# A soft mixture of experts that combines from the dispatch's own exponentials, strip by strip

## The chip, the cores and the metric

The kernel runs on one core of one Trainium2 chip. The metric is the device time of one launch in microseconds (us), as a median over several runs; lower is better. The engines that matter here are TensorE (PE in the profile, its weight loads PEld), VectorE (DVE), ScalarE (ACT), GpSimd (POOL) and the sync engine's queue (SP), which issues nearly all DMA transfers.

## The reference

Attention with a window of 96 keys, 8 global keys and a linear distance bias, for 4 batches, 8 heads, 768 positions and head width 64, makes `x` of 3072 tokens by 512. The second half is a soft mixture of experts with 8 experts of 4 slots each:

```python
logits = x @ phi                              # [3072, 32]
d = np.exp(logits - logits.max(0, keepdims=True))
d /= d.sum(0, keepdims=True) + 1e-09          # dispatch: per slot, over tokens
slot_input = d.T @ x                          # [32, 512]
for e in range(E):
    h = np.maximum(slot_input[e] @ w1[e], 0.0)
    slot_out[e] = h @ w2[e]                   # [32, 512] in all
c = np.exp(logits - logits.max(1, keepdims=True))
c /= c.sum(1, keepdims=True) + 1e-09          # combine: per token, over slots
return c @ slot_out                           # [3072, 512]
```

Both softmaxes are taken over the same logits, once along each axis.

## The kernel before

**Order.** Everything is issued from one flat program. The attention phase is the list `ORDER` (L56), a hand-written order of small steps that are looked up by name and called one after the other (L845); each engine takes its instructions in that order. Behind it `last_dispatch` (L763), the expert layers and the combine follow in plain program order. Weights stream in through SP (`load_w`, L397) into 2,048-column places, as soon as what lay there is used up.

**Attention.** Sixteen units (batch, pair of heads) pass through scores, bias, exponential, a split into two fp16 parts, values and division. `tr` (L624) transposes the output, and `logits` (L647) multiplies it by `phi`.

**Strips.** The logits of one batch stand on the 128 partitions as four strips of 32 slots: strip `s` holds tokens `240 s` to `240 s + 239`, so `lsb` is 128 by 240 (the last strip has 48 tokens). Each batch ends with `strip_max`, `strip_exp` and `strip_sum` (L688 to L708): a running maximum per partition, `ex = exp(lsb - max)` with its sum, and the rescaling of earlier sums. `by_token` (L716) transposes both `ex` and the raw logits `lsb` into tokens by slots, 120 tokens at a time; `by_token_copy` moves the first for the dispatch, and `lnat_copy` (L729) keeps the second in `lnat` (120 by 32 groups by 32 slots) for the combine. `dispatch` (L740) accumulates `d.T @ x` per strip in `sacc`.

**Last dispatch.** For the last batch the same steps run without cover. The strips' maxima are brought together per slot (`m4`, `ft`), `zn` holds the factors that fold the four strips and normalise, and two groups of matmuls (L814) give the slots' inputs, which `put_slots` (L104) places in `sl`. Small filler matmuls (`warm`, L773) stand between.

**Experts.** `hidden` (L110) runs twice, for experts 0 to 3 and 4 to 7, four experts side by side in 32-column groups; VectorE and ACT meanwhile run `softmax` (L154) over `lnat` and `split` (L166), which lays each weight out twice, as an F32R part and its remainder. `hidden_t` (L126) transposes the hidden rows, `weights_by_slot` (L175) transposes the split weights into `ct` (128 by 3072), and `check_inputs` (L860) works out whether the fast path's assumptions on the inputs hold. `project` (L141) multiplies by `w2`, for the two halves of 256 output columns one after the other, each over experts 0 to 3 and 4 to 7. Its result has 4 experts in 32-row groups, and each slot's row stands several times; `slots_out` (L191) folds the sign pattern `sgn` into an F32R part and a remainder, so that one matmul with `ct` gives the full product. `set_flag` (L879) sums the checks by a matmul into a flag that a branch at the end reads (L939); if it is set, a general path recomputes everything.

**Combine.** `Moe.combine` (L197) takes 128 tokens at a time: one F32R matmul of 128 rows by 256 columns (L209), two of them to a PSUM bank, evacuated in turn by ACT (L212) and VectorE (L214), and written to HBM in pieces of 4 tiles (512 KB) from six output buffers used in rotation. PSUM tiles of this stage rotate through six banks (`LeftBanks`, L500). The end of the program is

```python
    project(0, 0)
    project(0, 1)
    slots_out(0)
    set_flag()
    project(1, 0, range(3))
    combine(0, 0, (4,) * 5)
    project(1, 0, range(3, 8))
    project(1, 1)
    slots_out(1)
    combine(0, 20, (4,))
    combine(1, 0, (4,) * 6)
```

## Time and profile before

| what | value |
|---|---|
| median of 3 runs | 214.49 us (213.32 to 215.28) |
| the profiled execution | 213.26 us |
| its span, first to last instruction | 211.5 us |
| PE busy | 182.5 us, 86% |
| DVE / ACT / POOL busy | 150.8 / 127.6 / 116.0 us |
| moved by DMA | 61.40 MB, mean 290 GB/s |
| written to HBM | 6.29 MB |

The span is shorter than the profiled execution's own time by what lies around it. Times inside the span are counted from its start. The page's strip of 40 slices gives the busy share of 5.3 us each in tenths; that of TensorE shows it busy through nearly the whole span and idle in the last two slices:

```profile
PE   8679799986999989999999998887699999998400
```

In a row of the costliest groups the order is: line, engine, operation, output and inputs by the program's names, shapes, count, then busy time and the mean time of one in ns, then the engine's idle time ahead of them and what ended it. A piece of the chain of waits is: start, length, engine, tile and line, and the number of instructions merged in it. A window's row is: its ends and length, busy time of PE, PEld, DVE, ACT and POOL with counts, the granted TensorE clock, the mean share of the DMA engines, and GB/s. A matmul in fp32 shows as two records, an F32R matmul or a transpose as one.

### The profile page before, as it was taken

Reading aid. Unit: us, or ns where it says so; the run is one execution under the profiler, and the core shown is the slowest. Engines: PE = TensorE matmul, PEld = TensorE weight load, DVE = VectorE, ACT = ScalarE, POOL = GpSimd, SP = SyncE. Lnnn points to the kernel's source line nnn. Section 1 sums busy time; section 2 is a strip of 40 time slices with the busy share of each in tenths; the row PEclk is TensorE's granted clock in tenths of the full one; section 3 lists DMA queues with packets and bytes.
Section 4 is the critical chain, followed back from the end, with each engine's and each line's share of the span. In section 5 each row is a group of like instructions: output and inputs, shape, how many; then the busy total and the mean of one; then the engine's idle time right before and its main releaser. Section 6 shows DMA issues by size and latency. Waiting matters only on the chain.

```text
span 211.5 us, 6475 instructions
## 1 busy us (share of the span) xinstructions
PE 182.5 (86%) x2649; PEld 131.8 (62%) x2649; DVE 150.8 (71%) x375; ACT 127.6 (60%) x177; POOL 116.0 (55%) x141
## 2 busy tenths in 40 slices
PE   8679799986999989999999998887699999998400
PEld 2357688765787868878788876656253366576300
DVE  4889999658889878989988999296567835153600
ACT  2429899919589768979799989642403552042400
POOL 8436989785799796998889999840000000000000
PEclk9999999998899999999999999699999999999955
DMA  4769999997998976663487678998998999459892
GB/s 115 295 193 396 397 381 380 319 343 282 336 398 314 354 291 222 240 236 118 153 276 243 223 248 248 354 373 309 369 384 275 385 397 388 163 188 315 285 337 91
DMA packets 21063, 61.40 MB, mean 290 GB/s; under 512 B 2336, under 2 KB 9376, under 8 KB 19360
## 3 DMA queue, kind: packets, MB, share of 16 engines
q1 hardware_dynamic: 20880, 60.89, 79.8%
q8 instruction: 23, 0.38, 0.7%
q14 instruction: 16, 0.13, 0.2%
q10 hardware_dynamic: 144, 0.00, 0.0%
HBM read 54.59 MB, written 6.29 MB: 288 GB/s over the span
## 4 chain that ended last, share of the span: by engine, by line
PE 49%; DMA 18%; DVE 15%; POOL 9%; issue 3%; ACT 1%; DVEq 0%; POOLq 0%; SPq 0%
DMA wa<-in_v_dram 11%; PE x L602 11%; PE sc L538 9%; PE a L149 7%; PE hp L119 7%; POOL wa L586 6%; DVE wa L527 4%; PE m L631 3%; DMA wa<-in_qk_dram 3%; DVE wa L548 3%; PE m L736 2%; DMA out_dram<-wa 2%; DMA nraw<-in_n_dram 2%; POOL wa L519 2%; PE m L661 2%
## 5 line engine op out<-in xcount | busy, mean ns | idle before, releaser
L586 POOL TENSOR_TENSOR wa<-wa 128x432 f16<-128x432 f32 x91 | 98.4, 1111 | 12.3 <-ACT wa L578 8.1
L538 PE MATMUL sc<-wa 64*128 64x216 f32 (+2 forms) x448 | 49.3, 347 | 3.6 <-DVE mx L548 2.2
L602 PE MATMUL x<-wa 128*128 128x65 f16 (+1 forms) x1248 | 45.9, 196 | 3.5 <-POOL wa L586 2.0
L602 PEld LDWEIGHTS <-wa 128*128 128x128 f16 x1248 | 41.7, 99 | 9.6 <-issue 5.2
L578 ACT CAST wa<-wa 128x1296 f16<-128x1296 f32 x31 | 39.3, 1266 | 9.1 <-PE x L602 8.2
L538 PEld LDWEIGHTS sc<-wa 64*128 64x128 f32 x448 | 37.6, 190 | 10.6 <-DVE mx L548 4.1
L568 ACT ACTIVATE wa<-wa,nb 128x1296 f32<-128x1296 f32 x32 | 43.5, 1374 | 0.5
L548 DVE CUSTOM_DVE_ANT_1 wa<-sc,wa,mx 128x864 f32<-128x864 f32 x32 | 35.6, 1114 | 3.5 <-PE sc L538 1.0
L527 DVE SCALAR_TENSOR_TENSOR wa<-wa 128x896 f16<-128x896 f32 x16 | 24.3, 1519 | 5.5 <-ACT wa L522 3.1
L548 DVE CUSTOM_DVE_ANT_1 wa<-sc,wa 128x864 f32<-128x864 f32 x16 | 16.8, 1051 | 2.6 <-POOL wa L586 1.9
L636 ACT COPY wa<-m 128x480 f32<-128x480 f32 (+1 forms) x32 | 14.3, 473 | 6.7 <-PE m L631 6.7
L212 ACT COPY wa<-cp 128x512 f32<-128x512 f32 x12 | 6.3, 596 | 17.0 <-PE cp L209 15.3
L619 DVE CUSTOM_DVE_ANT_1 xn<-x,rc 120x448 f32<-120x448 f32 x24 | 14.9, 622 | 0.7
L522 ACT ACTIVATE wa<-wa 128x896 f16<-128x896 f32 x8 | 7.6, 951 | 11.4 <-DMA wa<-in_v_dram 10.5
L631 PE MATMUL m<-ident,xn 120*128 120x120 f32 x84 | 12.9, 276 | 1.1 <-DVE xmax L619 0.5
L519 POOL TENSOR_SCALAR wa<-wa 128x896 f16<-128x896 f32 x8 | 7.5, 941 | 10.7 <-DMA wa<-in_v_dram 8.4
L631 PEld LDWEIGHTS m<-ident,xn 120*128 120x128 f32 x84 | 8.6, 140 | 3.2 <-ACT wa L636 1.5
L119 PE MATMUL hp<-wp,sl 128*32 128x512 f32 x96 | 10.5, 593 | 0.0
L661 PE MATMUL m<-wa,phis 128*32 128x240 f32 (+1 forms) x128 | 9.5, 332 | 0.2 <-ACT wa L636 0.2
L214 DVE COPY wa<-cp 128x512 f32<-128x512 f32 x12 | 7.5, 682 | 2.1 <-PE cp L209 1.2
L609 DVE TENSOR_TENSOR rsall<-x,eps 120x7 f32<-120x7 f32 x32 | 5.0, 157 | 5.3 <-PE x L602 4.9
L561 PEld LDWEIGHTS m<-mm,bsel 2*128 2x128 f32 x32 | 4.7, 182 | 5.6 <-DVE mm L558 3.1
(163 smaller groups left out, 207.8 us busy)
## 6 DMA issues: line engine op xcount, KB each, us to landing
wa<-in_qk_dram SPq DMA_DIRECT2D x15, 832.0 KB, 6.6
wp<-in_w_dram SPq DMA_DIRECT2D x12, 1024.0 KB, 7.9
wa<-in_v_dram SPq DMA_DIRECT2D x16, 448.0 KB, 3.9
out_dram<-wa SPq DMA_DIRECT2D x12, 512.0 KB, 5.6
wp<-in_w_dram SPq DMA_DIRECT2D x8, 512.0 KB, 7.3
wp<-in_w_dram SPq DMA_DIRECT2D x16, 256.0 KB, 5.7
wa<-in_w_dram SPq DMA_DIRECT2D x3, 432.0 KB, 4.9
wa<-in_w_dram SPq DMA_DIRECT2D x1, 1024.0 KB, 6.8
```

The lines of the kernel that those rows point to most:

```text
L119: nc.tensor.matmul(out=hp[n][32 * s:32 * s + 32, :], lhsT=slv(a, c, s), rhs=w1(e, c // 2)[:, (c % 2) * DF + 512 * n:(c % 2) * DF + 512 * n ...
L149: nc.tensor.matmul(out=o[32 * s:32 * s + 32, 0:w], lhsT=ht[:, c, 32 * s:32 * s + 32], rhs=w2(4 * a + s, half)[:, c0 + c * w:c0 + c * w + w ...
L527: nc.vector.scalar_tensor_tensor(out=vlo[k].rearrange(flat), in0=vraw.rearrange(flat), scalar=V_SC, in1=vhi[k].rearrange(flat)[:, :, 0:D], ...
L538: nc.tensor.matmul(out=sc[:, i, at:at + n], lhsT=r_[r, KCOL[j]:KCOL[j] + KR], rhs=r_[r, KW + KB * j:KW + KB * j + n], start=True, stop=True)
L548: nc.vector.tensor_tensor_reduce(out=tbs[u % NTB].rearrange("p (i c) -> p i c", i=2)[:, :, BW * k:BW * k + BW], in0=scs.pop((u, k))[:, :, ...
L568: nc.scalar.activation(out=head(u, i), in_=head(u, i), func=AF.Exp, bias=nbs[u], scale=T_SC)
L578: nc.scalar.copy(out=h, in_=t)
L586: (engine or nc.gpsimd).tensor_tensor(out=w, in0=t, in1=h, op=ALU.subtract)
L602: nc.tensor.matmul(out=x[:, (D + 1) * t:(D + 1) * t + d], lhsT=w[:, c:c + P], rhs=vv[:, j, i, 0:d], start=(z == 0), stop=(z == len(ops) - ...
L619: nc.vector.tensor_tensor_reduce(out=xnb[(u // 2) % 3][:, :, c:c + D], in0=out_of(u, i)[:, :, 0:D], in1=rcs.pop((u, i)).unsqueeze(2).to_br ...
L631: nc.tensor.transpose(out=m[:, at:at + KB], in_=xnb[(u // 2) % 3][:, t, P * (p % 2):P * (p % 2) + P], identity=ident[0:KB, 0:KB])
L636: nc.scalar.copy(out=xtb[u % 3][:, a:a + n], in_=ms.pop((u, k))[:, 0:n])
```

## The change

The combine no longer has weights of its own. The exponentials `ex` of every batch are kept (`exs`, one strip tile of 128 by 240 for each batch), with the running maxima in `amax`. In `last_dispatch` the maximum over all partitions is found (`gmax`, through one transposing matmul and a reduce, and spread to all partitions by another matmul), each batch's strips are scaled by `exp(amax - gmax)` in place, and eight matmuls with a 128 by 4 selector `quad` give each token's sum over the 32 slots; their reciprocals `crec` later divide the output. Softmax by token, `split`, `weights_by_slot`, `ct` and `lnat` go. `slots_out` becomes two half copies by VectorE and ACT, and a new `slots_spread` multiplies by a permutation matrix `perm` so that every row group of 32 holds the 32 slots. The combine then takes each batch's strips as they stand: seven fp32 matmuls with 32 rows, one for each group of 120 tokens, four of them in different row groups and different PSUM banks. The evacuation multiplies by the reciprocals: VectorE for strips 0 and 2, ACT for strips 1 and 3. There are eight output buffers, one for each half and batch. `check_inputs` tests the sums in place of the softmax, and moves from behind `weights_by_slot` to behind the second `slots_spread`, with `set_flag` after it.

```diff
-    lnat = keep.tile([KB, 8 * B, NS], F32, name="lnat")
+    amax = keep.tile([P, B], F32, name="amax")
+    exs = [keep.tile([P, SW], F32, name=f"ex{b}") for b in range(B)]
...
+        nc.gpsimd.memset(quad, 0.0)
+        for k in range(4):
+            nc.gpsimd.memset(quad[32 * k:32 * k + 32, k:k + 1], 1.0)
+        nc.gpsimd.tensor_copy(out=perm.rearrange("p (r s k) -> p r s k", r=4, s=4), in_=ident.rearrange("p (s r k) -> p r s k", r=4, s=4))
...
     def by_token(b):
         ms[b, "d"] = m = bank()
-        to_tokens(m, ex, 0)
-        to_tokens(m, lsb, 2 * P)
+        to_tokens(m, exs[b], 0)
...
         strip_max(last)
         strip_exp(last)
-        ml = tile()
-        to_tokens(ml, lsb, 2 * P)
+        top = amax[:, b:b + 1]
+        nc.tensor.matmul(out=mt[0:1, 0:P], lhsT=top, rhs=ident, start=True, stop=True)
         warm()
...
+        nc.vector.tensor_reduce(out=gmax, in_=mt[0:1, 0:P], axis=AX.X, op=ALU.max)
+        nc.tensor.matmul(out=mt[:, P:P + 1], lhsT=ones[0:1, :], rhs=gmax, start=True, stop=True)
         for s in range(4):
             nc.vector.tensor_reduce(out=ft[32 * s:32 * s + 32, 0:1], in_=m4, axis=AX.X, op=ALU.max)
...
         by_token_copy(last)
-        ms[b, "d"] = ml
-        lnat_copy(last)
+        nc.vector.tensor_tensor(out=fs[:, 0:B], in0=amax, in1=mt[:, P:P + 1].to_broadcast([P, B]), op=ALU.subtract)
+        nc.scalar.activation(out=fs[:, B:], in_=fs[:, 0:B], func=AF.Exp)
+        for i in range(B):
+            f = fs[:, B + i:B + i + 1]
+            if i == 1:
+                nc.gpsimd.tensor_scalar(out=exs[i], in0=exs[i], scalar1=f, scalar2=0.0, op0=ALU.mult, op1=ALU.add)
+            else:
+                nc.scalar.activation(out=exs[i], in_=exs[i], func=AF.Copy, scale=f)
...
+        def sums(i):
+            for k in range(2):
+                at = 8 * i + 4 * k
+                nc.tensor.matmul(out=mc[0:KB, at:at + 4], lhsT=exs[i][:, KB * k:KB * k + KB], rhs=quad, start=True, stop=True)
+
+        sums(0)
+        sums(1)
         for g in range(2):
             m = tile()
             for c in (2 * g, 2 * g + 1):
                 nc.tensor.matmul(out=m[:, NS * c:NS * c + NS], lhsT=sacc[:, P * c:P * c + P], rhs=zn, start=True, stop=True)
-            if g == 0:
-                warm()
+            sums(2 + g)
             moe.put_slots(sl, m[:, 2 * NS * g:2 * NS * g + 2 * NS], 2 * g, 2 * g + 2)
+        nc.vector.tensor_scalar(out=csum, in0=mc[0:KB, 0:8 * B], scalar1=C_EPS, scalar2=None, op0=ALU.add)
+        nc.vector.reciprocal(out=crec, in_=csum)
...
-        reduced(7, KB, cst[:, :, 1], AX.X, 0.5)
+        reduced(0, KB, csum.rearrange("p (n s) -> p n s", s=4)[:, :, 0:3], AX.XY, C_MIN)
+        reduced(7, TN[6], csum[0:TN[6]].rearrange("p (b n) -> p b n", b=B)[:, :, 3], AX.X, C_MIN)
...
-    moe.softmax(lnat, cst, lnat)
...
-            for b in range(B):
-                moe.split(lnat[:, 8 * b:8 * b + 8], sps[b])
...
-    for b in range(B):
-        moe.weights_by_slot(left, sps[b], ct, [(4 * (t % 2) + t // 2, TN[t], S * b + KB * t) for t in range(NJ)])
-    check_inputs()
...
+    def halves(out, in_):
+        w = HF // 2
+        nc.vector.tensor_copy(out=out[:, 0:w], in_=in_[:, 0:w])
+        nc.scalar.copy(out=out[:, w:], in_=in_[:, w:])
...
     def slots_out(n):
+        c = slice(HF * n, HF * n + HF)
+        halves(ohs[:, c], ops[n][:, 0:HF])
+
+    def slots_spread(n):
+        spread[n] = m = left.tile([P, 512], F32, name="so", tag="x")
+        nc.tensor.matmul(out=m[:, 0:HF], lhsT=perm, rhs=ohs[:, HF * n:HF * n + HF], start=True, stop=True)
+        halves(sots[:, HF * n:HF * n + HF], m[:, 0:HF])
+
+    def combine(n, b):
...
+        cps = [left.tile([P, 512], F32, name="cp", tag="x") for _ in range(4)]
+        for k in range(2):
+            for s in range(4):
+                t = 2 * s + k
+                if t < NJ:
+                    nc.tensor.matmul(out=cps[s][0:TN[t], w * k:w * k + w], lhsT=exs[b][32 * s:32 * s + 32, KB * k:KB * k + TN[t]],
+                                     rhs=sots[32 * s:32 * s + 32, at:at + w], start=True, stop=True)
...
+        for s in (0, 1, 2, 3):
+            if s in (0, 2):
+                nc.vector.tensor_tensor(out=ob[:, 2 * s:2 * s + 2], in0=cps[s][0:KB].rearrange("p (k f) -> p k f", k=2),
+                                        in1=rec[:, s].unsqueeze(2).to_broadcast([KB, 2, w]), op=ALU.mult)
+            else:
+                for t in range(2 * s, min(2 * s + 2, NJ)):
+                    k, r = t - 2 * s, TN[t]
+                    nc.scalar.activation(out=ob[0:r, t], in_=cps[s][0:r, w * k:w * k + w], func=AF.Copy, scale=rec[0:r, s, k:k + 1])
+        if b == 0:
+            rows(0, 2)
+            rows(2, 6)
+        else:
+            rows(0, 6)
+        rows(6, 7)
...
     project(0, 0)
     project(0, 1)
     slots_out(0)
-    set_flag()
-    project(1, 0, range(3))
-    combine(0, 0, (4,) * 5)
-    project(1, 0, range(3, 8))
-    project(1, 1)
-    slots_out(1)
-    combine(0, 20, (4,))
-    combine(1, 0, (4,) * 6)
+    project(1, 0, (0,))
+    slots_spread(0)
+    project(1, 0, (1, 2))
+    combine(0, 0)
+    combine(0, 1)
+    project(1, 0, range(3, 8))
+    project(1, 1, (0,))
+    combine(0, 2)
+    project(1, 1, range(1, 8))
+    slots_out(1)
+    combine(0, 3)
+    slots_spread(1)
+    check_inputs()
+    set_flag()
+    for b in range(B):
+        combine(1, b)
```

`ORDER` differs only by the three `lnat_copy` steps, which go. `rows(t0, t1)` issues one write of those token groups on SP.

More of the change, by code (lines that the diff above doesn't have):

```diff
@@ L853, in tile_attention_moe @@
     ts = tail.enter_context(tc.tile_pool(name="ts", bufs=1))
-    ct = ts.tile([P, B * S], F32R, name="ct")
-    ohs = ts.tile([P, DM], F32R, name="ohs")
-    sots = ts.tile([P, DM], F32R, name="sots")
+    ohs = ts.tile([P, DM], F32, name="ohs")
+    sots = ts.tile([P, DM], F32, name="sots")
     fl = keep.tile([P, 12], F32, name="fl")
-    cst = keep.tile([KB, 8 * B, 4], F32, name="cst")
     def check_inputs():
```

46 lines of the change are left out of this document (25 added, 21 removed).

## Prediction

> **What bounds the kernel now.** I read the windows of the last 60 us first, then the chain of waits over the same stretch, then the rows of the instructions that the change adds to or takes from it. The chain of the end, as it stands:
>
> ```profile
> 155.50 0.56 PE ld L814 x4
> 156.06 0.37 PE a L775 x3
> 156.43 0.56 PE ld L814 x4
> 156.99 13.87 PE hp L119 x128
> 170.86 1.90 PE htp L133 x16
> 172.75 3.67 PE ctp L183 x28
> 176.42 0.21 PE xt L869
> 176.63 8.38 PE a L149 x148
> 185.01 2.59 PE cp L209 x20
> 187.59 5.79 PE a L149 x104
> 193.41 0.49 DVE ohs L194
> ...
> 195.08 4.12 DMA out_dram<-wa
> ```
>
> From 155.5 to 193.4 TensorE does one piece after the other without a gap: the path is its instruction order, and whatever is taken out of that order is gained and whatever is put into it is paid. At 193.4 the path leaves TensorE: sign folding on VectorE, one evacuation, and from 195.08 the queue of output writes. How that queue stands, per microsecond (busy time by engine, then granted clock, DMA share, GB/s):
>
> ```profile
> 181.00:182.00 1.00, 1.00 (x27) 0.57 (x23) 0.00 (x0) 0.00 (x0) 0.00 (x0) 1.00 0.83 297
> 182.00:183.00 1.00, 1.00 (x24) 0.63 (x20) 0.00 (x0) 0.00 (x0) 0.00 (x0) 1.00 0.18 66
> ...
> 195.00:196.00 1.00, 1.00 (x11) 1.00 (x10) 0.70 (x3) 0.88 (x2) 0.00 (x0) 1.00 0.28 75
> ...
> 200.00:201.00 1.00, 0.00 (x0) 0.00 (x0) 0.00 (x1) 0.00 (x0) 0.00 (x0) 1.00 1.07 344
> 201.00:202.00 1.00, 0.00 (x0) 0.00 (x0) 0.00 (x0) 0.00 (x0) 0.00 (x0) 0.88 1.02 322
> ...
> 207.00:208.00 1.00, 0.00 (x0) 0.00 (x0) 0.00 (x0) 0.00 (x0) 0.00 (x0) 0.50 0.50 172
> ```
>
> The weights are in by 182, well ahead of their use. After 195 the writes run near 340 GB/s and stop at about 207.5; the span's last 4 us follow the last write and do not change. So the end is: when the first write of the second output half starts (195.08), about 0.7 us until bytes flow (75 GB/s in that first window is 0.2 us of full rate), then the remaining bytes. Seven writes of 512 KB are left then: six of the second half and the last of the first.
>
> **The change part by part.** Ahead of 150 us three pairs of logit transposes and three ACT copies to `lnat` go. Only one pair stands in the chain, half of this piece:
>
> ```profile
> 100.87 0.59 PE m L713 x4
> ```
>
> I take -0.3 us. The POOL constants (`quad`, `perm`) cost nothing: POOL idles in front of its table work; without that cover they would cost some 1.7 us, six rows like the first one below.
>
> ```profile
> 5.77 0.28 POOL L478 TENSOR_TENSOR i<-i,ident 128x32 f32<-128x32 f32 x1
> ...
> 9.25 3.34 POOL L289 TENSOR_SCALAR wa<-wa 128x1728 bf16<-128x1728 bf16 x2 [2.93 <-DVE wa L283]
> ```
>
> Last dispatch. The maximum over all slots puts one DVE reduce ahead of the exponential that ACT needs before it copies the dispatch weights: 0.28 us by the first row below. The scaling of four strips (three on ACT, one on POOL) starts when those copies are out, some 0.5 us each by the second row, and ends near 155.5, before TensorE asks for it. The eight `sums` matmuls do lie on TensorE's path: each is two records, as the fp32 matmuls of L814 are (eight records for four), whose rows are:
>
> ```profile
> L558 DVE TENSOR_REDUCE mm<-m 1x1 f32<-1x128 f32 x16 | 4.4, 276 | 1.3 <-PE m L555 0.8
> L697 ACT ACTIVATE ex<-lsb,al 128x240 f32<-128x240 f32 x4 | 2.0, 495 | 3.1 <-DVE al L692 1.9 <-POOL al L692 1.3
> ...
> L814 PE MATMUL ld<-zn,sacc 128*128 128x32 f32 x8 | 1.3, 281 | 0.0
> ```
>
> ```profile
> 155.43 0.63 PE L814 MATMUL ld<-zn,sacc 128*128 128x32 f32 x4
> ```
>
> Four records span 0.63 us and the last one alone is 0.28, so a start follows a start after 0.12 us. Sixteen records: 1.9 us. The ends are 0.5 us (0.033 us, the record of the attention values in this piece, far away)
>
> ```profile
> 90.57 1.30 PE x L602 x39
> ```
>
> and 2.24 us (0.56 us per four, the chain's own price); I take 1.9, the same shape of weights. One filler of 0.37 us goes (L775). Stage: 0.28 + 1.9 - 0.37 = +1.8 us.
>
> Then the transposes of the combine weights (L183) and the check's transpose (L869) leave the path ahead of the second projection: -3.88 us. Softmax, split and the first minimum were VectorE and ACT work beside the 13.87 us of L119 and give nothing. So the projections start at 176.63 - 0.3 + 1.8 - 3.88 = 174.25. The weights' transfer shifts later with `hidden`, by 1.5 us, and is still in before it is used.
>
> Combine. Each (half, batch) is now seven fp32 matmuls of 32 rows in four row groups instead of six F32R ones on 128 rows. A 256-column pass costs 13.87 us / 32 / 2 = 0.217 us by L119 (four column groups side by side). Two row groups side by side are in the scores:
>
> ```profile
> 84.76 0.93 PE sc L538 x8
> ```
>
> ```profile
> L538 PE MATMUL sc<-wa 64*128 64x216 f32 x320 | 41.8, 375 | 3.6 <-DVE mx L548 2.2 <-DMA wa<-in_qk_dram 1.2
> ```
>
> Eight records of 216 columns (0.183 us a pass by the same rate) would be 1.46 us one after the other and 0.73 in pairs; 0.93 says pairs. If four groups do as well, a combine is four steps of 0.217 plus a little, 1.0 us; singly it would be 3.04 us. The Trainium skill ("TensorE: Matmul & The Clock Gate", "Part 3: Packing small matmuls — row/col tiling") gives 3.07 times for four row tiles, measured at 512 columns; by it the block is 0.99 us as an estimate and the sum stays. The same section says that matmuls start and end in strict order, which would make the second pass of a block hold up the next row group; L119's 13.87 us speak against that for column groups.
>
> Evacuation per block: two VectorE products and three ACT copies, by
>
> ```profile
> L173 DVE TENSOR_TENSOR wp<-lnat,wp 120x512 f32<-120x512 f32 x4 | 2.5, 683 | 0.7 <-ACT wp L172 0.7
> L726 ACT COPY dn<-ld 120x256 f32<-120x256 f32 x1 | 0.4, 353 | 0.0
> ```
>
> 1.4 us and 1.1 us: less than the 2.31 us that 786 KB take at 340 GB/s, so the writes remain the limit once they run. The sync queue issues nine transfers per half in place of six; by
>
> ```profile
> L215 SPq DMA_DIRECT2D out_dram<-wa x12: 372/1010/2187, 186.5 to 202.9; - x12
> ```
>
> an issue takes 0.37 us when the rings have room (the median is 1.01, of a queue that is full), 3.3 us for nine, beside 9.25 us of bytes. But a block takes four of the six banks, so the second of two blocks in a row waits for the first one's VectorE product: the pair is 1.0 + 0.8 + 1.0 = 2.8 us. Between the end of the first projection and the end of the second TensorE gets the spread (two passes and a short wait, 0.5), the pair and one block: 4.3 us in place of 2.59. End of the second projection: 193.39 - 2.4 + 1.7 = 192.7.
>
> From there the order by hand is what costs. VectorE takes the half copy (its 0.48 us product is gone), then the two products of block (0,3) whose matmuls come first, then the copy of the spread slots, and then all of `check_inputs`; TensorE has the flag matmul of `set_flag`, which needs the last of these, ahead of the first combine of the second half. Before, the checks stood beside the first projection:
>
> ```profile
> 176.83 0.34 DVE L863 TENSOR_REDUCE fl<-rsall 120x1 f32<-120x192 f32 x1
> ...
> 177.95 0.19 DVE L863 TENSOR_REDUCE fl<-cst 120x1 f32<-120x32 f32 x1
> 178.18 0.15 DVE L864 TENSOR_SCALAR fl<-fl 120x1 f32<-120x1 f32 x1
> ...
> 178.74 0.15 DVE L877 TENSOR_SCALAR fl<-fl 128x1 f32<-128x1 f32 x1
> ```
>
> 2.06 us, and one more reduce with its compare, 0.34: 2.4 us. In time: block (0,3) ready 192.7 + 1.0 + 0.15 = 193.85; two products, 195.25; copy of the spread, about 0.3, 195.55; checks, 197.95; flag matmul 0.2; first block of the second half 1.15, 199.3; one product, 200.0; first write. Its bytes flow 0.7 later, 3.15 MB at 340 GB/s take 9.25: 209.95. Block (0,3) was written from 196 to 198.3, so the queue stands empty for some 2.4 us. Against 207.5: **+2.45 us**. The removed wait for output buffers (six places become eight) gives nothing, since it was a wait for a full queue.
>
> The profiled execution took 213.26 us, so it would take 215.7. It is the fastest of the runs shown; the median is 214.49, 1.23 above it. As a median I forecast **216.9 us**.
>
> **The rivals.** *Not slower.* The checks do not lie in the path, because their VectorE work runs while it would wait anyhow. Then the first write of the second half comes at 197.6, while (0,3) is still being written; the queue never empties, five blocks run from 196 and end at 207.55: 214.5 us. It decides from 0.3 us less than my 2.4 on, since the measurement tells about 1% (2.1 us) from no change. For it: the write of (0,3), 2.31 us, is about as long as the checks. Against it: in the trace these VectorE rows stand in the order in which the program issues them, and nothing on that engine is due between.
>
> *Half clock.* From the last spread to the first combine TensorE idles about 4 us. Before, its last matmul ended at 197.75 and the clock fell at 201.76 (0.88 in that window, 0.50 after), 4 us later:
>
> ```profile
> 194.75 3.00 PE L209 MATMUL cp<-sots,ct 128*128 128x256 f32 x23
> ```
>
>  If it falls ahead of the first block, that block takes twice its 0.9 us; later blocks still keep up with 2.31. 217.8 us. The Trainium skill (same page, "Part 1: The HAM clock gate (the "warmup" mystery)") has the clock halve after an idle window of about 3.4 us; by that rule this rival would be the forecast, while the trace has it on the edge.
>
> *Fewer row groups at once.* If two passes in one group hold up the next, a block is 1.9 us: +1.7 for the pair, +0.9 each for the third, for (0,3) and for (1,0): +4.4, 221.3 us. L538 speaks for pairs and cannot show four.
>
> **How the numbers follow.** Forecast 0.53, own range 215.4 to 218.2 (sums 0.5 to 2.24 us, the pair with or without its wait, attention 0 to -0.9); of that 0.23 lies within 1%. Not slower 0.18, at 214.5. Half clock 0.16, 217.8. Fewer row groups 0.07, 221.3. Some 0.06 is left for a gain that I don't see in the attention stages. Faster by over 1% (below 212.3): 0.06. Within 1%: 0.23 + 0.18 = 0.41. Slower (above 216.6): 0.30 + 0.16 + 0.07 = 0.53. The range 214.2 to 220.5 leaves out the gain, most of the fewest row groups and the lower edge of the second case.
>
> **What would show it.** No L183 piece; `sums` as 16 records of about 0.12 us; L119 some 1.5 us later; the projections some 2.4 us earlier; block combines of about 1 us with four records starting together; a stretch from 195.5 to 198 in which VectorE does checks and TensorE nothing; windows near 199 with hardly any GB/s. I am wrong if the writes of the second half start before 198.3, if the combine blocks are 2 us or longer, or if `sums` hide.

## The result, and the profile after

The change takes 232.44 us (median of 4 runs, 229.85 to 233.83) against 213.91 us (212.75 to 215.28) for the kernel before on the same chip: a ratio of 1.0823, 95% interval 1.0699 to 1.0947. Forecast were 216.9 us and a range up to 220.5. The sign is right, the size is far off: +18.5 us in place of +2.4. Ratios here and below leave out disturbed runs, so one can differ from the quotient of the medians beside it.

The page of the changed kernel: the span, busy time, and from the strip of 40 slices (5.76 us each) TensorE, its granted clock, and the bytes moved.

```profile
span 230.4 us, 6579 instructions
...
PE 200.2 (87%) x2698; PEld 134.9 (59%) x2698; DVE 142.4 (62%) x369; ACT 127.1 (55%) x184; POOL 118.5 (51%) x148
...
PE   8678899894999999999998978779999999859910
...
PEclk9999999999799999999999979999999988955555
...
GB/s 132 244 251 408 347 406 370 355 349 398 302 241 328 265 317 202 125 230 212 214 240 255 214 363 356 315 365 273 295 391 392 368 103 190 139 139 139 168 201 57
```

TensorE is now busy almost to the end, and in the last five slices at half its clock; the writes of the second half move 139 to 201 GB/s a slice until they end, where they ran near 340 before. TensorE's timeline of the changed kernel shows where the time went (start, length, line, tiles, shapes, count; in brackets the idle time before and what ended it):

```profile
151.83 0.38 PE L789 MATMUL ld<-ident,amax 128*1 128x128 f32 x2 [1.04 <-DVE amax L690]
...
156.52 1.00 PE L831 MATMUL a<-quad,ex 128*120 128x4 f32 x8
157.38 0.61 PE L838 MATMUL ld<-zn,sacc 128*128 128x32 f32 x4
157.83 0.56 PE L831 MATMUL a<-quad,ex 128*120 128x4 f32 x4
158.25 0.61 PE L838 MATMUL ld<-zn,sacc 128*128 128x32 f32 x4
158.70 0.56 PE L831 MATMUL a<-quad,ex 128*120 128x4 f32 x4
159.19 10.51 PE L121 MATMUL hp<-wp,sl 128*32 128x512 f32 x96
...
174.96 7.11 PE L151 MATMUL a<-wa 128*32 128x256 f32 x128
...
187.07 1.88 PE L956 MATMUL cp<-sots,ex 32*120 32x256 f32 x10 [0.34 <-DVE wa L967]
188.88 4.46 PE L151 MATMUL a<-wp,wa 128*32 128x256 f32 x48
193.27 1.89 PE L956 MATMUL cp<-sots,ex 32*120 32x256 f32 x14
195.09 3.23 PE L151 MATMUL a<-wp,wa 128*32 128x256 f32 x56
198.24 1.89 PE L956 MATMUL cp<-sots,ex 32*120 32x256 f32 x14
...
204.02 0.19 PE L905 MATMUL ft<-ones,fl 128*1 128x1 f32 x2 [3.15 <-DVE fl L901]
204.14 15.78 PE L956 MATMUL cp<-sots,ex 32*120 32x256 f32 x56
```

Up to 175 us all is as reckoned: the sums (L831) are 16 records in 1.77 us, and between `hidden` (L121) and the projections (L151) the transposes of the combine weights are gone. From there on each block of the combine (L956, 14 records) takes 1.82 us to the start of what follows, and the last four take 15.78 us together. One piece of the second projection, 48 records from 188.88 on, takes 4.39 us to the next start: the clock was at half there. VectorE's products (L967) give the period of the last four blocks:

```profile
207.54 1.29 DVE L967 TENSOR_TENSOR wa<-cp,crec 120x512 f32<-120x512 f32 x2 [3.15 <-PE cp L956]
211.67 1.29 DVE L967 TENSOR_TENSOR wa<-cp,crec 120x512 f32<-120x512 f32 x2 [2.85 <-PE cp L956]
...
219.94 1.29 DVE L967 TENSOR_TENSOR wa<-cp,crec 120x512 f32<-120x512 f32 x2 [2.85 <-PE cp L956]
```

Every 4.13 us one block, and VectorE waits for TensorE 2.85 us of it. The windows of that time (columns as in the prediction: granted clock, DMA share and GB/s are the last three) show the queue of writes running dry between blocks:

```profile
202.00:204.00 2.00, 0.00 (x0) 0.01 (x1) 1.67 (x14) 0.00 (x0) 0.00 (x0) 0.63 0.74 147
...
206.00:208.00 2.00, 2.00 (x11) 1.13 (x10) 0.46 (x1) 0.42 (x2) 0.00 (x0) 0.50 0.08 22
...
212.00:214.00 2.00, 2.00 (x7) 0.70 (x4) 0.96 (x2) 0.90 (x3) 0.00 (x0) 0.50 0.19 50
...
222.00:224.00 2.00, 0.00 (x0) 0.00 (x0) 0.00 (x0) 0.00 (x0) 0.00 (x0) 0.50 0.87 188
224.00:226.00 2.00, 0.00 (x0) 0.00 (x0) 0.00 (x0) 0.00 (x0) 0.00 (x0) 0.50 0.81 239
```

The last two rows are a second loss: no block is due any more, the transfer engines are busy for 0.81 to 0.87 of the time, and still move only 188 and 239 GB/s; before, a share of 1.07 moved 344. By the traces' packet records a packet of 1 KB (256 values, one half of an output row) took 49.6 ns on the mean before and 66.0 ns here.

The start of `hidden` lies anywhere from 154.8 to 162.4 us in the profiles of the kernels below, and part of that is half-clock windows which come in some executions and not in others. So the traces are compared by stretches from the start of the projections; a stretch ends where its last record starts. In those terms, from before to after: start of the projections 176.56 to 174.96 (-1.6); from there to the end of the second projection 16.40 to 22.98 (+6.6); from that to the last packet 15.64 to 28.15 (+12.5). Together 17.5 of the 18.9 us that the span grew; 1.4 more lie behind the last packet.

### The profile page after: what moved, and what is told of

Same layout as the page of the kernel before. It is cut to its first block, busy times and chain, and to the rows that moved or that the text cites. A ratio compares the mean times of both kernels' runs of the same rounds, so it can differ in the third digit from the quotient of the medians.

```text
span 230.4 us, 6579 instructions
## 1 busy us (share of the span) xinstructions
PE 200.2 (87%) x2698; PEld 134.9 (59%) x2698; DVE 142.4 (62%) x369; ACT 127.1 (55%) x184; POOL 118.5 (51%) x148
## 4 chain that ended last, share of the span: by engine, by line
## 5 line engine op out<-in xcount | busy, mean ns | idle before, releaser
L539 DVE SCALAR_TENSOR_TENSOR wa<-wa 128x896 f16<-128x896 f32 x16 | 23.4, 1460 | 4.8 <-POOL wa L531 4.2
L956 PE MATMUL cp<-sots,ex 32*120 32x256 f32 (+1 forms) x112 | 23.7, 547 | 0.3 <-DVE wa L967 0.3
L967 DVE TENSOR_TENSOR wa<-cp,crec 120x512 f32<-120x512 f32 x16 | 10.3, 686 | 22.0 <-PE cp L956 22.0
L972 ACT ACTIVATE wa<-cp,crec 120x256 f32<-120x256 f32 (+1 forms) x24 | 9.5, 467 | 24.4 <-PE cp L956 24.4
L956 PEld LDWEIGHTS cp<-sots,ex 32*120 32x120 f32 (+1 forms) x112 | 10.0, 224 | 13.4 <-issue 7.2
L121 PE MATMUL hp<-wp,sl 128*32 128x512 f32 x96 | 10.5, 593 | 0.0
L141 DVE COPY wa<-htp 128x512 f32<-128x512 f32 x2 | 1.4, 691 | 14.2 <-PE htp L135 14.2
```

The source lines that it names most:

```text
L121: nc.tensor.matmul(out=hp[n][32 * s:32 * s + 32, :], lhsT=slv(a, c, s), rhs=w1(e, c // 2)[:, (c % 2) * DF + 512 * n:(c % 2) * DF + 512 * n ...
L539: nc.vector.scalar_tensor_tensor(out=vlo[k].rearrange(flat), in0=vraw.rearrange(flat), scalar=V_SC, in1=vhi[k].rearrange(flat)[:, :, 0:D], ...
L956: nc.tensor.matmul(out=cps[s][0:TN[t], w * k:w * k + w], lhsT=exs[b][32 * s:32 * s + 32, KB * k:KB * k + TN[t]], rhs=sots[32 * s:32 * s + ...
```

## The experiments

Theory at the start: a block is long because its seven matmuls don't run four abreast, the tail is long because the clock stays at half, and the writes are slow because 120 rows go at a time. Rivals: the clock falls because of the idle time that the input checks make; the fourth row group is slow by itself; the writes wait for something else. The stretches (us, each from one profiled execution) and the packets stand in one table; a time without a ratio is of a single execution. Beside the first four edits below the kernel before was run once, and took 218.69 us, so their times can't be set against 213.91 us; the stretches are what is read there. The profiled execution of "both, with fillers" took 224.03 us:

| kernel | projections to last packet | end of 2nd projection to last packet | mean 1 KB packet, ns | time, ratio to before |
|---|---|---|---|---|
| before | 32.0 | 15.6 | 49.6 | 213.91 |
| the change | 51.1 | 28.2 | 66.0 | 232.44, 1.082 |
| checks early | 49.2 | 26.2 | 66.1 | 227.90 |
| last strip 120 | 40.9 | 21.9 | 61.4 | 218.49 |
| both of these | 40.7 | 21.6 | 62.1 | 216.93, 1.036 |
| both, with fillers | 40.0 | 20.9 | 61.9 | 221.62, 1.028 |
| 128 columns, split writes | 37.7 | 18.8 | 54.9 | 219.82, 1.048 |
| 128 columns, 6 x 128 rows written | 36.2 | 17.3 | 49.4 | 214.72, 1.010 |
| before, 120 of 128 rows written | 32.2 | 15.8 | 53.6 | 214.67 |

**Checks early.** Is the half clock the price of the idle time in front of the first block?

```diff
+    check_inputs()
     project(0, 0)
     project(0, 1)
     slots_out(0)
+    set_flag()
...
     slots_spread(1)
-    check_inputs()
-    set_flag()
     for b in range(B):
```

> The input checks and the flag matmul go back to where they stood before the change: checks ahead of the first projection, flag behind the first slots_out. Theory A (the wait for the checks leaves TensorE idle, the clock falls in that gap and is not regained): no gap, the clock stays at 1.00 through the second half's blocks, a block of the second half takes 1.8 us instead of 4.1, and the time falls by 2.4 + 4 x 2.3 = about 11 us, to some 221. Theory B (the row-tiled blocks themselves do not count as a busy TensorE): the clock falls all the same within the last blocks and stays at 0.50, they still take about 4.1 us each, and only the wait of 2.4 us goes: about 230.

```profile
198.68 15.35 PE L956 MATMUL cp<-sots,ex 32*120 32x256 f32 x56 [1.29 <-ACT sots L933]
```

```profile
198.00:202.00 4.00, 3.32 (x18) 1.65 (x18) 0.67 (x3) 0.58 (x3) 0.00 (x0) 0.65 0.70 163
202.00:206.00 4.00, 4.00 (x18) 1.83 (x14) 1.15 (x3) 1.06 (x4) 0.00 (x0) 0.50 0.79 206
```

TensorE idles only 1.29 us ahead of the blocks. In its windows the clock falls at about 199 us all the same and stays at 0.50, and a block still takes some 4 us. So the wait for the checks is not the cause. In the tail the checks cost 2.0 us (28.2 to 26.2).

**Last strip 120.** The matmul of the last strip has 48 weight columns (48 tokens), the six others 120. Here it gets 120, 72 of them to no use:

```diff
-                    nc.tensor.matmul(out=cps[s][0:TN[t], w * k:w * k + w], lhsT=exs[b][32 * s:32 * s + 32, KB * k:KB * k + TN[t]],
+                    nc.tensor.matmul(out=cps[s][0:KB, w * k:w * k + w], lhsT=exs[b][32 * s:32 * s + 32, KB * k:KB * k + KB],
```

> The matmul of the last strip, which has 48 tokens, is given 120 weight columns like the others (the 72 further output rows are not used). Theory: the odd size of 48 is why it runs alone, so that a block is three steps. Then four records start together and a block is two steps: 1.25 us instead of 1.82 at full clock, 2.5 instead of 3.7 at half clock, and the time falls by about 4 x 1.2 + 4 x 0.6 = 6 to 7 us, to some 226. Rival: row group 3 itself cannot run beside the others: still three steps, no change (232).

The same block in the changed kernel (TensorE and its weight loads from 198.24 on), and then in this one:

```profile
198.24 0.29 PEld L956 LDWEIGHTS cp<-sots,ex 32*120 32x120 f32 x6 [0.41 <-issue]
198.24 1.89 PE L956 MATMUL cp<-sots,ex 32*120 32x256 f32 x14
...
198.87 0.16 PEld L956 LDWEIGHTS cp<-sots,ex 32*48 32x48 f32 x2 [0.34 <-issue]
199.43 0.29 PEld L956 LDWEIGHTS cp<-sots,ex 32*120 32x120 f32 x6 [0.40 <-issue]
```

```profile
187.11 1.13 PE L956 MATMUL cp<-sots,ex 32*120 32x256 f32 x14
188.17 3.23 PE L151 MATMUL a<-wp,wa 128*32 128x256 f32 x56
...
196.47 9.28 PE L956 MATMUL cp<-sots,ex 32*120 32x256 f32 x56
```

In the changed kernel three groups' weights are loaded, then those of the 48 columns 0.63 us later, then three more after 0.56: three steps one after the other. With equal widths there is no break; the block is 1.06 us to the next start, and the tail's four take 9.28 in place of 15.78. More work, 10 us less from the projections to the last packet (51.1 to 40.9). So neither the number of row groups nor the fourth one is at fault, but the odd width (and with it the 48 output rows, which the edit changes too). (The Trainium skill, "TensorE: Matmul & The Clock Gate", "Part 3: Packing small matmuls — row/col tiling", has 3.07 times for four row tiles; 14 passes of 0.217 in 1.06 us are 2.9 times, near it, and with the odd width 1.82 us are 1.7 times.)

**All 128 rows.** Every matmul contracts over all 128 partitions of strips and slots, which sums the four strips' products: the output is another than the reference's.

```diff
-                    nc.tensor.matmul(out=cps[s][0:TN[t], w * k:w * k + w], lhsT=exs[b][32 * s:32 * s + 32, KB * k:KB * k + TN[t]],
-                                     rhs=sots[32 * s:32 * s + 32, at:at + w], start=True, stop=True)
+                    nc.tensor.matmul(out=cps[s][0:TN[t], w * k:w * k + w], lhsT=exs[b][:, KB * k:KB * k + TN[t]],
+                                     rhs=sots[:, at:at + w], start=True, stop=True)
```

> Each combine matmul runs over all 128 rows instead of the 32 of its strip, so that the output is not the reference's (every token group sums over all four strips); the number and size of the matmuls stay. Nothing can run side by side: 14 passes of 0.217 us make a block 3.0 us at full clock, 6.1 at half. Theory B: with all rows in use the clock stays at or returns to 1.00 in the tail, a block takes 3.1 to 3.3 us, less than the 4.1 of the row-tiled block, and the time falls by 2 to 4 us in the tail but loses 4 x 1.3 ahead of it: 230 to 234, with the granted clock near 1.00 behind 206 us. Theory A: the clock stays at 0.50 as before, a block takes 6 us and the time rises by 10 us or more, to 243.

```profile
214.00:218.00 4.00, 4.00 (x11) 2.35 (x10) 0.69 (x1) 0.36 (x1) 0.00 (x0) 0.57 0.22 57
218.00:222.00 4.00, 4.00 (x19) 2.84 (x18) 1.78 (x3) 1.66 (x6) 0.00 (x0) 1.00 0.74 180
```

With matmuls on all 128 rows in the tail the clock comes back to 1.00 at 217.85, after one window of 3.41 us at half. With seven of these in a row a block is 3.6 us, and the kernel took 240.55 us.

**112 rows written.** Of each group of 120 rows 8 stay unwritten.

```diff
-            o = out[a:a + r * (t1 - t0), at:at + w]
-            nc.sync.dma_start(out=o.rearrange("(t p) f -> p t f", p=r), in_=ob[0:r, t0:t1])
+            o = out[a:a + r * (t1 - t0), at:at + w].rearrange("(t p) f -> p t f", p=r)
+            m = r // 16 * 16
+            nc.sync.dma_start(out=o[0:m], in_=ob[0:m, t0:t1])
```

> The large writes take 112 of the 120 rows of each token group; the last 8 rows of each group are not written. Theory: the writes of 120 rows run at 180 to 290 GB/s, against 340 before, because the rows do not divide by 16; with 112 rows most 1 KB packets take 46 to 48 ns again and the rate while the queue is full is 320 GB/s or more. The time falls little, since TensorE is the limit in the tail: by 0.5 to 1 us. Rival: the rate follows from the source's strides or the mix with the small writes: the packets stay as slow as they are.

233.49 us: the blocks hold the tail, so the time shows nothing. The packets are shorter, 57.1 ns on the mean against 66.0, but not at 49.6: only partly a matter of rows in sixteens.

**Both.** Early checks and 120 columns together.

> Both single edits together: the last strip's matmul has 120 weight columns, and checks and flag stand where they stood before the change. Theory: the two costs are separate, so the checks give their 2 us once more: the first write of the second half starts some 2 us earlier than with the 120 columns alone, and the time falls from 218.5 to about 216. Since the blocks at half clock (2.2 us) are as fast as the writes, the clock does not matter. Rival: the writes are the limit already, and the checks were covered by the write of block (0,3): 218.

216.93 us (216.08 to 219.58) against 211.81, a ratio of 1.036 (1.022 to 1.051) for 1.082: by these more than half of the loss is gone, at the upper end of the interval some two fifths, and not all. The input checks, which cost 2.0 us in the changed kernel, are worth 0.3 here (21.9 to 21.6).

**Double, fillers, quadruple: what the clock follows.** Three versions of the kernel with 120 columns. The first issues each matmul of the second half twice (back to back 3.23 us, then a wait of 0.66 for the bank); the second keeps them single and puts fillers of the kernel's own kind (all 128 rows, one weight column, 512 columns) behind each block; the third issues them four times. All three have the checks late, the third too, other than its expectation says.

```diff
-        for k in range(2):
+        for k in (0, 1, 0, 1) if n else (0, 1):
```

> With the 120 columns, every combine matmul of the second half is issued twice (the second one computes the same again), so that TensorE has hardly any waits between its row-tiled steps. It tells apart why the clock stays at 0.50 in the tail. Theory W (the waits of 0.66 us in a block of 2.2 are what keeps TensorE from counting as busy): with about 2.9 us of matmuls back to back a block, the clock returns to 1.00 within two windows of 3.4 us. Theory R (matmuls of 32 rows do not count as full work, whatever the waits): it stays at 0.50 to the end of the blocks, and a block takes 2.9 us, so that the time rises by about 3 us to 221.

```diff
+        if n:
+            for _ in range(4):
+                nc.tensor.matmul(out=idle[0:1], lhsT=busy_in[:, 0:1], rhs=busy_in, start=True, stop=True)
```

> With the 120 columns, four filler matmuls on all 128 rows (512 columns of bf16, one weight column, their result unused) stand behind the matmuls of each block of the second half: 0.85 us at full clock, 1.7 at half. Theory R and theory W both say that the clock returns to 1.00 within two windows, since the waits are filled with work on all rows; then a block is 1.05 + 0.85 us and the time stays within 1.5 us of 218.5. If the clock stays at 0.50, neither is right, a block is 3.2 us and the time rises by 4 us.

```diff
-        for k in range(2):
+        for k in (0, 1) * 4 if n else (0, 1):
```

> The version with 120 weight columns in every strip and early checks, with each matmul of the second half's blocks issued four times over (same result). The waits for the bank are then only about a tenth of each block. If the clock stays down because matmuls on 32 rows do not count as full work, it stays at 0.50 to the end, and a block takes some 7 us. If it stays down because of the waits in each block, it goes back to 1.00 within two windows, and a block takes some 3.7 us.

Doubled, the four blocks took 3.9 us each and the clock stayed at 0.50 to the end (227.43 us). With fillers it came back at 207.89, behind two windows (225.98 us). This spoke for a rule that matmuls on 32 rows don't count. The fourfold version refutes that (its windows):

```profile
198.00:201.40 3.40, 2.25 (x21) 1.97 (x24) 1.01 (x10) 0.00 (x0) 0.00 (x0) 0.51 0.84 202
201.40:204.80 3.40, 3.40 (x32) 2.83 (x31) 0.00 (x0) 0.00 (x0) 0.00 (x0) 0.50 0.03 9
204.80:208.00 3.20, 2.85 (x41) 2.22 (x40) 1.29 (x2) 1.19 (x3) 0.00 (x0) 0.99 0.18 32
```

There is nothing on TensorE but matmuls on 32 rows, and after one full window of them the clock is back.

**Fillers in the change itself.** The same four fillers, 48 columns and late checks left as they are.

> The change itself with four filler matmuls of 512 columns on all 128 rows behind each block of the second half; nothing else differs. It prices the half clock in the real change. If the clock stays down because matmuls on 32 rows do not count as full work, it is back at 1.00 within two windows of 3.41 us after the first block with fillers, and a block goes from 4.13 us to about 2.7 to 2.9 us (1.82 of strips and 1.0 of fillers at full clock): about 5 us less than the change. If the clock stays at 0.50, each block pays the fillers as well, some 4 to 7 us more than the change.

```profile
204.85 3.38 PE L956 MATMUL cp<-sots,ex 32*120 32x256 f32 x14
208.16 1.87 PE L960 MATMUL a<-const-bfloat16-1.0 128*1 128x512 bf16 x4
```

The clock was expected back and did not come: TensorE has no idle time at all from 199.75 on, yet the clock stays at 0.50. So being busy isn't enough either; the section on the hardware takes this up. From the projections to the last packet pass 55.1 us for 51.1 in the change, so the fillers were paid; the time, 232.32 us, is that of the change only since this execution's projections began at 170.55, 4.4 us earlier. What the half clock costs in the changed kernel was thus not measured by itself.

**128 columns, split writes.** Blocks of 128 weight columns that overlap by 16 tokens, so that the first group of a strip is written from 128 rows and the second from 112; early checks, and one VectorE copy in place of the two half copies.

```diff
+            for k in range(2):
+                nc.sync.dma_start(out=o[P * k:P * k + P - 16 * k, s0:s1], in_=ob[16 * k:P, 2 * s0 + k:2 * s1:2])
```

> All together, with writes of 128 rows: token groups start at 0 and 112 of a strip and every combine matmul has 128 weight columns, so that the first group of each strip is written from 128 rows and the second from the last 112; the checks stand early, and one VectorE copy takes the place of the two half copies. Theory: the writes of 120 rows run at 180 to 300 GB/s because of the row count; with 128 and 112 rows the full queue moves 300 or more, the second half's 3.15 MB take 10.5 us instead of 12 and the time falls to about 214, at or a little under the kernel before. Rival: the row count is not the reason, and the time is that of checks_early_120.

**Reordered.** The same, with all rows of both groups written (16 of them twice) and all four blocks of the first half ahead of the second half's slots.

```diff
-                nc.sync.dma_start(out=o[P * k:P * k + P - 16 * k, s0:s1], in_=ob[16 * k:P, 2 * s0 + k:2 * s1:2])
+                nc.sync.dma_start(out=o[112 * k:112 * k + P, s0:s1], in_=ob[:, 2 * s0 + k:2 * s1:2])
```

> A version meant to beat both: every strip's matmul has 128 weight columns, the input checks come before the first projection, blocks of both token groups are written from all 128 rows (16 rows at each strip's edge are written twice with the same values), all four blocks of the first half lie between the pieces of the second projection, and the second half's blocks follow its copies at once. If writes of 128 rows go at the 340 GB/s of before and the blocks keep up (about 1.1 us at full clock, 2.2 at half, against 2.31 us of writing), the end follows the first write of the second half by 9.3 us and the time is 211 to 216 us, at or a little under before. If the half clock or the copies hold the blocks, it is 217 to 220 us, as the version with separate writes before it was.

The first one has shorter packets (54.9 ns) and takes 3 us less from the projections to the last packet than the version with 120 columns and early checks; its time, 219.82 us, is no better, with a ratio of 1.048 (1.034 to 1.062) beside 1.036 (1.022 to 1.051). In its profile the clock was at half from 157.2 to 164.0, in `hidden`, which makes up for the gain: 18.8 us from there to the projections, for 15.9. The second was meant to win and took 229.59 us, a ratio of 1.074 (1.067 to 1.081). Its packets are fine (50.1 ns); what holds it stands in the waits of the sync queue:

```profile
SPq L962 <- DMA out_dram<-wa: 21.3, 10, 3.3
```

Ten writes wait 21.3 us in all for an earlier write. The version with split writes, whose rows don't overlap, has no such wait, so the rows that are written twice are the likely reason that each waits for the landing of an earlier one. That is a fault of this version and says nothing of the change.

**What is left.** Two causes remained for the 3.6%: the half clock in the tail, and the writes. The kernel before with 120 of each 128 rows written, the rest left unwritten:

```diff
-                out=out[P * t0:P * (t0 + size), at:at + w].rearrange("(t p) f -> p t f", p=P), in_=ob.rearrange("p (t f) -> p t f", f=w))
+                out=out[P * t0:P * (t0 + size), at:at + w].rearrange("(t p) f -> p t f", p=P)[0:KB], in_=ob.rearrange("p (t f) -> p t f", f=w)[0:KB])
```

> The kernel before, but each block of the output is written from 120 of its 128 rows: the last 8 rows of every 128 are left unwritten. Nothing else differs, so it tells whether 120 rows by themselves make the writes slow. If the row count is the reason (the writes of the changed kernel go 120 rows each, with a mean 1 KB packet of 66 ns against 49.6 ns before), the mean 1 KB packet goes to some 60 ns or more and the windows with a full queue fall under 300 GB/s from 340; the end of the writes then moves by at most 2 us, since there are also 6% fewer bytes. If it is the order of the blocks or something else in the changed kernel, packets stay at about 50 ns and the time is that of before less up to 0.5 us.

214.67 us in one execution, against 212.57 us (211.63 to 212.99): 53.6 ns a packet, and the stretch to the last packet is 0.2 us longer with 6% fewer bytes. The row count alone slows the writes, but less than in the changed kernel. Then each cause taken away by itself: the version of 128 columns writes 6 x 128 rows without gaps or overlap, in wrong rows, and no longer a small write of 48 rows for each half and batch (10 writes in all, for 28 in the split version and 18 in that of 120 columns); and the version with 120 columns and early checks gets fillers that keep the clock up, behind the spread as shown and behind each block as before.

```diff
-            for k in range(2):
-                nc.sync.dma_start(out=o[P * k:P * k + P - 16 * k, s0:s1], in_=ob[16 * k:P, 2 * s0 + k:2 * s1:2])
+            o = out[S * b + P * t0:S * b + P * t1, at:at + w]
+            nc.sync.dma_start(out=o.rearrange("(t p) f -> p t f", p=P), in_=ob[:, t0:t1])
...
-        nc.sync.dma_start(out=out[S * b + 3 * SW:S * b + S, at:at + w], in_=ob[0:LAST, 6])
```

> The version with separate writes (checks early, 128 weight columns in every strip), but each block is written as 6 x 128 rows without gaps, the pattern of the kernel before: as many bytes, in wrong rows. Nothing else differs. If the writes of fewer than 128 rows are what is left of the loss, the mean 1 KB packet goes from 54.9 ns back to about 49 ns, a full queue moves 340 GB/s, and from the end of the second projection to the last packet pass some 15 to 16.5 us in place of 18.8; the time falls by 2 to 3 us. If the blocks or the half clock hold the tail, the writes have gaps in place of that and the time stays.

```diff
     slots_spread(1)
+    idle = left.apart(0)
+    for _ in range(4):
+        nc.tensor.matmul(out=idle[0:1], lhsT=busy_in[:, 0:1], rhs=busy_in, start=True, stop=True)
```

> The version with 120 weight columns in every strip and early checks, with four filler matmuls of 512 columns behind the spread of the second half and behind each of its blocks, so that the clock should stay at 1.00 to the end of the matmuls. If the half clock costs time there (blocks of 2.19 us at half against 1.13 at full), the tail from the end of the second projection to the last packet falls from 21.6 us by 2 us or more, and the time below 215 us beside a kernel before of 211.8. If the writes of 120 rows at some 255 GB/s hold it, as the full queue from 184 us on says, the tail and the time stay within 1 us or so of that version, whatever the clock.

Windows of the version with 120 columns and early checks, then of the one with fillers, of the one that writes 128 rows, and of the split writes:

```profile
196.00:200.00 4.00, 4.00 (x32) 2.66 (x26) 2.37 (x4) 2.18 (x6) 0.00 (x0) 0.50 0.91 246
200.00:204.00 4.00, 1.77 (x10) 0.93 (x9) 1.65 (x3) 1.39 (x4) 0.00 (x0) 0.50 0.90 223
204.00:208.00 4.00, 0.00 (x0) 0.00 (x0) 0.00 (x0) 0.00 (x0) 0.00 (x0) 0.50 0.94 276
```

```profile
204.00:208.00 4.00, 4.00 (x37) 1.91 (x36) 2.53 (x5) 2.35 (x6) 0.00 (x0) 1.00 0.87 231
208.00:212.00 4.00, 0.91 (x4) 0.17 (x2) 1.27 (x2) 1.19 (x3) 0.00 (x0) 1.00 0.93 226
```

```profile
196.00:200.00 4.00, 4.00 (x28) 2.86 (x28) 2.20 (x4) 2.00 (x7) 0.00 (x0) 0.52 0.92 302
200.00:204.00 4.00, 2.34 (x13) 1.25 (x10) 2.20 (x4) 1.94 (x6) 0.00 (x0) 0.50 1.03 337
```

```profile
200.00:204.00 4.00, 3.29 (x35) 2.02 (x31) 3.00 (x5) 2.76 (x8) 0.00 (x0) 1.00 0.99 296
208.00:212.00 4.00, 0.00 (x0) 0.00 (x0) 0.00 (x0) 0.00 (x0) 0.00 (x0) 0.55 0.98 295
```

With the clock at 1.00 through all blocks the writes go no faster, and the ratio of 1.028 (1.018 to 1.038) can't be told from 1.036 (1.022 to 1.051). That alone shows little, since a block and its fillers still take 2.02 us, for 2.19 at half clock. The other windows show more. With 120 columns TensorE's last block ended at 201.8, and the writes went on for 10 us. With split writes the clock was at 1.00 and a block took 1.68 us, and the queue held the tail at 295 GB/s. With writes of 128 rows the full queue is at 337 GB/s while the clock is at 0.50 and a block takes 2.19 us. So with equal widths the half clock costs nothing that can be measured, and the writes hold the tail. Most of their part goes with the row count: the split writes, which keep the small ones, take 3.0 of the 4.5 us away (128 columns and the single copy included); the last 1.5 came with the 128 rows and the smaller number of writes together.

The ratio of the last version is 1.0096 (1.0056 to 1.0137). Not all of the step from 1.048 is the writes': its program and that of the split writes are the same up to the writes, and yet its profile has the projections at 171.81 us and the other at 176.88, with 3.4 us at half clock ahead of them in the one and 10.2 in the other. By the stretches the writes are 1.5 us of it.

No version beat the kernel before.

## Why the prediction was wrong, point by point

- **Last dispatch, +1.8 us: right.** From the first matmul behind the strips' maxima to `hidden` pass 159.19 - 151.83 = 7.36 us; before, 5.88 (from 151.04). That is +1.5. The sums took 1.77 for 1.9. The -0.3 in the attention didn't show: that first matmul came 0.8 us later than before, in one execution each, which settles nothing.
- **L183 and L869, -3.88 us: right.** From `hidden` to the projections 15.77 us in place of 19.64: -3.87.
- **"four steps of 0.217 plus a little, 1.0 us": the step that failed.** The prediction counted matmuls and row groups and not their widths. Four groups do run side by side, as it argued from the scores, but those all have the same shape. With 48 columns among 120 the block is 1.82 us at full clock; with equal widths it is 1.06, and that alone took 10.2 us off the way to the last packet. The rival of fewer groups at once, at 0.07, had nearly this block (1.9) by another mechanism, and its 221.3 us lacked all that follows below.
- **"later blocks still keep up with 2.31": failed with it.** The half clock rival doubled 0.9 us for one block. The clock did fall, at 202.5, and a block of 1.82 us and a wait became 4.13; four of them run past the writes. With equal widths the clock fell in some profiles too (at 195.32 in that of 120 columns and early checks), and there that sentence holds: 2.2 us a block. The half clock came in the projection as well (4.39 us for the 48 records that take 2.73 with equal widths, +1.7), which was not reckoned with.
- **Writes at 340 GB/s: mis-sized.** The prediction took the rate of a full queue from writes of 128 rows and carried it over to 120. They ran at 223 to 276 GB/s with equal widths. Taking this away is worth 21.6 - 17.3 = 4.3 us in the last stretch, the 128 columns and the smaller number of writes included.
- **The checks: right in size, 2.25 us of VectorE work for 2.4,** and the wait stood where it was put (TensorE idle 3.15 us until L901). They cost 2.0 us in the tail. The rival that they don't lie in the path is nearly true only where the writes hold the tail (0.3 us).
- **"the span's last 4 us follow the last write and do not change": they did.** From the last packet to the end pass 2.9 us before and 4.3 in the change, +1.4. In the other profiles it is anything from 1.9 to 5.2; what sets it was not looked into.
- **The sum.** From the projections to the last packet, in the order in which the parts were taken away: widths 10.2 us, checks 0.2 behind that, the writes 4.5 (40.7 to 36.2), and 4.2 that stay against before. Of these 4.2, 2.5 stand ahead of the end of the second projection, where the prediction had +1.7 for the spread and the blocks; 1.7 stand behind it, where the queue ran dry (17 GB/s from 193 to 194 us in the version that writes 128 rows) though the checks were early. The front gives back 3.9 - 1.5 = 2.4, so 1.8 us are left, and a ratio of 1.0096 says 2.0. That this is near the prediction's +2.45 is luck: its +2.45 stands on the wait for the checks, and the version that is left at +2.0 has no such wait.

## What to carry to other kernels

Before matmuls in different row groups are reckoned as side by side, see that they have the same number of weight columns; pad the odd one, since here work that ran abreast was cheaper than a shorter piece that ran alone. Only 48 beside 120 was tried, so how near the widths must be isn't shown. A write rate is read from transfers with the same number of rows, and a block that just keeps up with its writes has to be reckoned at half the clock as well. After a fix, measure the next limit again: the checks were worth 2.0 or 0.3 us, depending on what held the tail.

## What the runs showed of the hardware

- **Unequal widths side by side.** 120, 120 and 120 columns ran together, 48 alone: 0.63, 0.56 and 0.63 us in place of 1.06 for all.
- **What the clock follows.** In tails of TensorE work the granted clock came back from 0.50 in three kernels (blocks on all 128 rows, blocks with fillers, fourfold blocks) and not in the change, with doubled blocks, in the change with fillers, or in the others whose single blocks ran at half. One measure fits all of them, as an estimate made after the runs: how much of the time all 128 rows of the array are at work. A block's 14 passes of 32 rows make 3.5 passes of 128, 0.217 us at full clock and twice that at half, so 1.52 us; four fillers, which have all rows and one weight column, took 1.80. That gives 1.52 of 4.13 = 37% in the change, 1.52 of 2.19 = 69% in single blocks of equal widths, (1.52 + 1.80) of 5.1 = 65% in the change with fillers, 3.04 of 3.9 = 78% doubled, and where it came back (1.52 + 1.80) of 3.80 = 87% with fillers, 6.08 of 6.9 = 88% fourfold, and all of the time in blocks on 128 rows. No kernel was made to test it, so it stays open. It says nothing on when the clock falls: the versions of split writes and of 6 x 128 rows have the same matmuls in the same order, and in the one profile the clock stayed at 1.00 until 208.42, behind the last block, in the other it fell at 196.14, ahead of most of them. The Trainium skill (same page, "Part 1: The HAM clock gate (the "warmup" mystery)") has the clock come back after one busy window of about 3.4 us; the fourfold version agrees (one window, 201.4 to 204.8), while the change with fillers was without idle time from 199.75 to the end of its matmuls and stayed at half, and there the measurement decides.
- **Writes of fewer than 128 rows.** Packets of 1 KB went from 49.6 ns (128 rows) to 53.6 (120 of each 128), 54.9 (128 and 112), 57.1 (112 of each 120) and 61 to 67 (120 after 120). With a full queue the transfer engines were busy for 0.90 to 0.94 of the time at 120 rows and 1.03 at 128. The row count is part of it; why 120 after 120 is the slowest was not found out.
